# Weights' products ahead of what waits for VectorE within an attention step, and products of a zero tile where there are none

## The chip, the cores and the metric

One core of a Trainium2 chip runs the whole program in one launch. TensorE (PE) does the matrix products and transposes, VectorE (DVE) and ScalarE (ACT) read their results from PSUM, GpSimd (POOL) and SyncE (SP) issue the transfers. The metric is the device time of one execution in microseconds; 916.21 is the median of three runs of the kernel before (915.81 to 922.91).

## The reference

Three pieces run one after the other. First an attention over 2 x 8 heads of 768 positions and 64 dimensions, in which a query sees only the keys whose six signs under a random projection agree with its own:

```
mask   = q_bucket[:, :, :, None] == k_bucket[:, :, None, :]
scores = np.where(mask, scale * q @ k.T, -1e9)
attn   = exp(scores - max) ; attn = attn / (sum(attn) + 1e-09) ; out = attn @ v
```

Its output, 1536 x 512, goes through x = (h * tanh(softplus(h))) @ w_out with h = x @ w_in (2048 wide), and then through ((x @ w1) * (x @ w2)) @ w3 @ w_out (1024 wide). The last two matrices are multiplied with one another by the kernel (w3 @ w_out), and this product doesn't depend on the attention.

## The kernel before, in words

All products run on fp32 split into a high and a low part, in three passes. The attention is a loop over 96 steps n (line 865), pinned in the order in which it is written (`pin`, line 830). Six steps, n = 6j to 6j + 5, make one half pair of heads j; below, the position of a step is n mod 6. A step does the scores of one tile of 128 queries (`scores`, L540, tile ts, two PSUM banks), the row maximum (`maxima`, L551 and L554, VectorE), the exponential (`expo`, L562, ScalarE), and, for the half pair before, transposes of the exponentials (`unit`, L605, tile et, copied to etf in L612 by either ScalarE or VectorE) and products with the values (`av`, L620, tile pv, positions 2 to 4).

Other work hangs in named slots of a step, filled with `at(n, slot, fn)` and emptied with `run(n, slot)` in the order of lines 868 to 886: "la" (ScalarE copies), "un" and "av", "lv" (VectorE work that frees a bank), then "pe", "ea", "ev", "dm". Slot "pe" holds on TensorE: `qk_transpose` (L470, tile tqk) at positions 2 and 3, `bits_mm` (L500, tile tb) at positions 4 and 5, `rb_mm` (L587, tile rb) and, from n = 24 to n = 66, `w3_trans` (L678, tile w3p) at position 0. The tiles ts, tqk, tb and w3p share one ring of two PSUM buffers (tag "s"), so a later one waits until an earlier one has been read: tb at position 5 waits for `bits_dve` (L509) of position 5 to read the tb of position 4. rb waits for the reciprocal of `norm` (L574, L577), which runs in slot "lv" behind the copies of et and behind L509.

The weights' products are `wp_mm` (L703, tile wacc, the product w3 @ w_out; n = 26 to 73; 2, 2, 1, 6, 4 and 9 products at positions 2, 3, 4, 5, 0 and 1) and `h_early` (L334, tile hps, the first products of h; from n = 83; 4 or 8 a step). Both sit in slot "pe" too, and both write the one bank of tag "w". In the steps 0 to 25, and 74 to 82, there are none. TensorE takes its instructions in the order written. Behind the loop comes the block phase: three blocks of 512 rows through both networks. In the first block the weights are loaded as 64-bit numbers, one MB a chunk, by transfers that GpSimd issues (`load64`, L81), decoded by ScalarE and VectorE (L89, L96, L99, L107), and written back for the later blocks (L218).

Of the kernel before, what the change touches and what calls it, by code (L numbers as in the profile page):

```python
# [18 lines left out]
F32 = mybir.dt.float32  # L19
FR = mybir.dt.float32r  # L20
# [14 lines left out]
def kernel(  # L35
# [14 lines left out]
    nc = tc.nc  # L50
# [14 lines left out]
    const = ctx.enter_context(tc.tile_pool(name="const", bufs=1))  # L65
    big = ctx.enter_context(tc.tile_pool(name="big", bufs=2))
    strm = ctx.enter_context(tc.tile_pool(name="strm", bufs=2))
    ps = ctx.enter_context(tc.tile_pool(name="ps", bufs=1, space=PSUM))
# [8 lines left out]
    identr = const.tile([128, 128], FR, tag="identr", name="identr")  # L77
# [250 lines left out]
    def h_half(n, j, f, o, m0=0, m1=None):  # L328
        w, xh = weight(n, "wi", j), xhl[n]
        m1 = 3 * KD if m1 is None else m1  # L330
        for m in range(m0, m1):
            kk, i = divmod(m, 3)
            ws, xs = PASS[i]
            nc.tensor.matmul(  # L334
                o, lhsT=w[:, ws, kk, f * 128:(f + 1) * 128], rhs=xh[xs][:, kk, :],
                start=(m == 0), stop=(m == 3 * KD - 1),
            )
# [14 lines left out]
    def h_early(n, j, f, m0, m1):  # L352
        if m0 == 0:
            wh[0] = ps.tile([128, 512], F32, tag="w", name="hps1")
        h_half(n, j, f, wh[0], m0, m1)
# [32 lines left out]

    nc.scalar.preload_act_table_set("natural_log_exp_and_others")
    make_identity(nc, ident)  # L390
    zr = strm.tile([128, 512], FR, tag="xi", name="zr", bufs=2)
    nc.vector.memset(zr.bitcast(F32), 0.0)
    nc.scalar.copy(out=identr, in_=ident)

# [128 lines left out]
    for r in range(3):  # L523
        t = pa.tile([128, 6, 6], F32, tag=f"st{r}", name="st", bufs=1)
# [24 lines left out]
    def maxima(j, i):  # L549
        s = stats[j % 3]  # L550
        nc.vector.tensor_reduce(  # L551
            out=s[:, i, 1:2], in_=sc[j, i][:, :, 0:HS], axis=AX.XY, op=ALU.max, negate=True
        )
        nc.vector.scalar_tensor_tensor(  # L554
            out=s[:, i, 2:4], in0=s[:, i, 1:2].to_broadcast([128, 2]), scalar=THR,
            in1=s[:, i, 0:2], op0=ALU.is_le, op1=ALU.mult,
        )
# [14 lines left out]
    def norm(j):  # L572
        s = stats[j % 3]
        nc.vector.tensor_scalar(  # L574
            out=s[:, :, 4], in0=s[:, :, 4], scalar1=1e-9, scalar2=None, op0=ALU.add
        )
        nc.vector.reciprocal(out=s[:, :, 5], in_=s[:, :, 4])  # L577
# [4 lines left out]
    def rb_mm(j):  # L582
        s = stats[j % 3]
        t = rbs[j] = ps.tile([128, 512], F32, tag="p", name="rb")
        for ci in range(CH):
            for e in range(2):
                nc.tensor.matmul(  # L587
                    t[e * D:(e + 1) * D, ci * 128:(ci + 1) * 128],
                    lhsT=s[:, e * CH + ci, 5:6].to_broadcast([128, D]),
                    rhs=ident, start=True, stop=True,  # L590
                )

    def rb_act(j):
        t = rbs[j]
        rbs[j] = pa.tile([128, HS], F32, tag="rb", name="rb", bufs=2)
        nc.scalar.copy(out=rbs[j], in_=t[:, 0:HS])
# [5 lines left out]
    def unit(j, e, kt):  # L602
        t = ps.tile([128, 512], F32, tag="et", name="et", bufs=2)
        for ci in range(CH):
            nc.tensor.transpose(  # L605
                t[:, ci * 128:(ci + 1) * 128],
                E[j, e * CH + ci][:, kt * 128:(kt + 1) * 128],
                ident,
            )
        f = pa.tile([128, HS], F32, tag="etf", name="etf", bufs=NR)  # L610
        act = kt % 2 == 0 or (e == 0 and kt == 3)
        (nc.scalar.copy if act else nc.vector.tensor_copy)(out=f, in_=t[:, 0:HS])  # L612
        eth[j, e, kt] = f

    def av(j, kt):
        p = j // 2
        if kt == 0:
            pv[j] = ps.tile([128, 512], F32, tag="p", name="pv")
        for e in range(2):
            nc.tensor.matmul(  # L620
                pv[j][e * D:(e + 1) * D, 0:HS],
                lhsT=raws[p, "v"][:, e, kt, :],
                rhs=eth.pop((j, e, kt)),
                start=(kt == 0),
                stop=(kt == C - 1),
            )

    def x_out(j):
        p, a = divmod(j, 2)
        b, hp = divmod(p, H // 2)  # L630
        o = pa.tile([128, HS], F32, tag="xo", name="xo", bufs=2)
        nc.vector.tensor_mul(out=o, in0=pv.pop(j)[:, 0:HS], in1=rbs.pop(j))
        c0 = b * S + a * HS
        nc.sync.dma_start(out=x_d[hp * 128:(hp + 1) * 128, c0:c0 + HS], in_=o)
        blocks_done.add((p, a))
# [16 lines left out]
    def pre_a(nm, i):  # L652
        pre[nm, i] = decode_a(pre[nm, i])

    def pre_b(nm, i):
        pre[nm, i] = decode_b1(pre[nm, i])

    def pre_c(nm, i):
        pre[nm, i] = decode_b2(pre[nm, i])
        x = PRE.index((nm, i)) + 2  # L660
        if x < len(PRE):
            pre_load(x)
# [34 lines left out]
    def wp_mm(f, n0, n1):  # L697
        if n0 == 0:
            wacc[f] = ps.tile([128, 512], F32, tag="w", name="wacc")
        for n in range(n0, n1):  # L700
            g, s = divmod(n, 3)
            ws, rs = PASS[s]
            nc.tensor.matmul(  # L703
                wacc[f], lhsT=w3t[f][:, ws, g, :], rhs=wo2[rs][:, g, :],
                start=(n == 0), stop=(n == 3 * GT - 1),
            )
# [6 lines left out]

    slots = {}

    def at(n, where, fn):
        slots.setdefault((n, where), []).append(fn)

    def run(n, where):
        for fn in slots.pop((n, where), []):
            fn()
# [28 lines left out]
    for j in range(NJ):  # L752
        s = 6 * j
        for m in range(3):
            for kt in (2 * m, 2 * m + 1):
                at(s + 4 + m, "un", lambda j=j, kt=kt: unit(j, 0, kt))
                at(s + 7 + m, "un", lambda j=j, kt=kt: unit(j, 1, kt))
                at(s + 8 + m, "av", lambda j=j, kt=kt: av(j, kt))
        at(s + 6, "lv", lambda j=j: norm(j))
        at(s + 6, "pe", lambda j=j: rb_mm(j))  # L760
        at(s + 7, "la", lambda j=j: rb_act(j))
        at(s + 11, "lv", lambda j=j: x_out(j))
# [7 lines left out]
    for f in range(GT):  # L770
        n = 24 + 6 * f
        na, nb, nc_ = (n - 6, n - 4, n - 3) if f else (17, 20, 21)
        at(na, "ea", lambda f=f: pre_a(3, f))
        at(nb, "ev", lambda f=f: pre_b(3, f))
        at(nc_, "ev", lambda f=f: pre_c(3, f))
        at(n, "pe", lambda f=f: w3_trans(f))
        at(n + 1, "la", lambda f=f: w3_hi(f))
        at(n + 1, "lv", lambda f=f: w3_lo(f))
        m = 0
        for k_ in range(n + 2, n + 8):  # L780
            m1 = m + MM[k_ % 6]
            at(k_, "pe", lambda f=f, m=m, m1=m1: wp_mm(f, m, m1))
            m = m1
        assert m == 3 * GT
        at(n + 8, "la", lambda f=f: wp_out(f))
# [20 lines left out]
    n = 83  # L806
    for jj in range(3):
        for f in range(2):
            m = 0
            while m < 12:  # L810
                m1 = min(12, m + (4 if n % 6 in (2, 3, 4) or n == 83 else 8))
                at(n, "pe", lambda jj=jj, f=f, m=m, m1=m1: h_early(0, jj, f, m, m1))
                m = m1
                n += 1
            at(n, "la", lambda jj=jj, f=f: h_keep(0, jj, f))
    HEND = n

    def warm(n):
        t = ps.tile([128, 512], F32, tag="p", name="warm")
        for _ in range(n):  # L820
            nc.tensor.matmul(t, lhsT=zr[:, 0:128], rhs=zr, start=True, stop=True)

    def keep_warm(n, src):
        t = ps.tile([128, 512], F32, tag="p", name="warm")
        for _ in range(n):
            nc.tensor.matmul(t[:, 0:HS], lhsT=identr, rhs=src, start=True, stop=True)
# [38 lines left out]
    for n in range(max(NS + 6, HEND + 2)):  # L865
        j, i = divmod(n, 6)
        mark = len(nc.cur_bb.bb.instructions)
        run(n, "pr")
        if n < NS:
            scores(j, i)  # L870
        run(n, "la")
        if n < NS:
            maxima(j, i)
        run(n, "un")
        run(n, "av")
        run(n, "lv")
        if n < NS:
            expo(j, i)
        if n == 0:
            for x in range(2):  # L880
                with tc.issue_after(next(
                    i for i in reversed(nc.cur_bb.bb.instructions) if i.engine == nc.scalar.engine
                )):
                    pre_load(x)
        for w in ("pe", "ea", "ev", "dm"):
            run(n, w)
        pin(mark)
# [164 lines left out]
```

## Time and profile before

| | us |
|---|---|
| median of three runs | 916.21 |
| profiled execution | 920.4 |
| its span, first to last instruction | 918.6 |
| steps 0 to 95 (attention) | about 12 to 450 of the span |
| block phase | about 450 to the end |

The profiled execution is one of its own, 4.2 us above the median. PE busy times are from modelled ends of pipelined products, so the start of the next instruction is the better mark for how long one takes; "idle before" names the stretch in which an engine had nothing running, with what released it. [...]

### The profile page before, as it was taken

What the parts mean: (1) busy time and instruction counts of PE and PEld (TensorE: products, weight loads), DVE (VectorE), ACT (ScalarE), POOL (GpSimd) and SP (SyncE); (2) the same over time, 40 slices, a digit from 0 to 9 for tenths busy, and PEclk for the clock granted to TensorE, in tenths of its full rate; (3) what the DMA queues carried; (4) which work ended last, traced back from release to release, by engine and by line L of the source; (5) the groups of instructions that cost most, each with busy time, mean ns of one, the idle gap of its engine ahead of it and who ended that gap; (6) DMA issues with size and microseconds to landing.
All of it is one profiled execution on the core that took longest, in us unless ns stands there. A gap on an engine that the chain in (4) does not pass through costs nothing.

```text
span 918.6 us, 10516 instructions
## 1 busy us (share of the span) xinstructions
PE 830.0 (90%) x4145; PEld 648.7 (71%) x4145; DVE 512.4 (56%) x711; ACT 459.9 (50%) x691; POOL 74.6 (8%) x131
## 2 busy tenths in 40 slices
PE   6778868888888898788999999999999999999998
PEld 4655656566666666556778778888888888888886
DVE  5477756666655756767689877432354434334321
ACT  4556645566645675657856554333344323334221
POOL 1000000000000000001022211100101101110000
PEclk8588979999999999999999999999999999999999
DMA  5112313131031331326098864424233224232101
GB/s 177 52 54 81 117 55 107 67 118 58 26 113 55 118 103 36 115 89 214 9 329 301 293 231 183 142 94 152 95 110 97 92 92 137 95 107 75 46 24 47
DMA packets 34594, 103.46 MB, mean 113 GB/s; under 512 B 3184, under 2 KB 11632, under 8 KB 33520
## 3 DMA queue, kind: packets, MB, share of 16 engines
q0 software_dynamic: 20928, 81.80, 26.3%
q1 hardware_dynamic: 13472, 20.85, 6.6%
q8 instruction: 33, 0.54, 0.2%
q14 instruction: 17, 0.14, 0.1%
q10 hardware_dynamic: 144, 0.13, 0.0%
HBM read 81.79 MB, written 20.97 MB: 112 GB/s over the span
## 4 chain that ended last, share of the span: by engine, by line
PE 71%; DVE 14%; issue 5%; DMA 5%; ACT 4%; POOL 1%; SPq 0%; ACTq 0%; DVEq 0%; POOLq 0%
PE abp L941 14%; PE hps L334 10%; PE x2a L914 10%; PE ts L540 8%; PE oac L965 7%; PE pv L620 6%; PE wacc L703 5%; DVE st L551 4%; PE et L605 4%; PE tb L500 3%; DMA raw<-in_moe_w_dram 2%; PE rb L587 2%; DMA raw<-in_moe_w_out_dram 2%; DVE qa L509 2%; DVE ka L509 2%
## 5 line engine op out<-in xcount | busy, mean ns | idle before, releaser
L551 DVE TENSOR_REDUCE st<-ts 128x1 f32<-128x768 f32 x96 | 91.9, 957 | 151.3 <-PE ts L540 151.3
L941 PE MATMUL abp<-x2hl,hl 128*128 128x512 f32 x576 | 139.3, 398 | 2.1 <-ACT mh L347 2.1
L334 PE MATMUL hps<-xhl,hl 128*128 128x512 f32 x552 | 135.8, 400 | 0.0
L914 PE MATMUL x2a<-ghl,hl 128*128 128x512 f32 x552 | 130.6, 394 | 1.2 <-DVE ghl L379 1.1
L941 PEld LDWEIGHTS abp<-x2hl,hl 128*128 128x128 f32 x576 | 109.4, 190 | 28.4 <-ACT mh L347 2.5
L269 DVE TENSOR_TENSOR hl<-f,hl 128x1024 fp32r<-128x1024 f32 x60 | 73.4, 1224 | 91.5 <-ACT hl L264 91.5
L334 PEld LDWEIGHTS hps<-xhl,hl 128*128 128x128 f32 x552 | 104.2, 191 | 26.6 <-issue 3.5
L914 PEld LDWEIGHTS x2a<-ghl,hl 128*128 128x128 f32 x552 | 103.6, 188 | 25.9 <-DVE ghl L379 2.0
L562 ACT ACTIVATE E<-ts,st 128x768 f32<-128x768 f32 x96 | 95.3, 993 | 27.9 <-DVE st L554 26.5
L612 ACT COPY etf<-et 128x384 f32<-128x384 f32 x112 | 51.9, 478 | 85.0 <-PE et L605 84.4
L605 PE MATMUL et<-ident,E 128*128 128x128 f32 x576 | 85.0, 287 | 0.0
L605 PEld LDWEIGHTS et<-ident,E 128*128 128x128 f32 x576 | 74.4, 149 | 4.5 <-ACT etf L612 0.2
L264 ACT CAST hl<-f 128x1024 fp32r<-128x1024 f32 x60 | 62.8, 1047 | 28.9 <-PE abp L941 12.0
L620 PE MATMUL pv<-etf,rv 128*64 128x384 f32 x384 | 74.5, 511 | 0.0
L540 PE MATMUL ts<-ka,qa 76*128 76x384 f32 x192 | 59.2, 393 | 12.7 <-ACT E L562 10.9
L965 PE MATMUL oac<-hl,phl 128*128 128x512 f32 x288 | 69.8, 393 | 0.0
L965 PEld LDWEIGHTS oac<-hl,phl 128*128 128x128 f32 x288 | 54.2, 188 | 12.4
L703 PE MATMUL wacc<-wo,w3t 128*128 128x512 f32 x192 | 56.8, 419 | 0.0
L950 DVE TENSOR_TENSOR asb<-abp,asb 128x512 f32<-128x512 f32 x24 | 16.6, 692 | 71.6 <-ACT asb L949 71.6
L949 ACT COPY asb<-abp 128x512 f32<-128x512 f32 x24 | 14.1, 586 | 83.9 <-PE abp L941 83.9
L89 ACT ACTIVATE g<-raw 128x1024 f32<-128x1024 f32 x36 | 41.0, 1140 | 28.5 <-DMA raw<-in_moe_w_dram 9.6
L540 PE MATMUL ts<-kb,qb 128*128 128x384 f32 x192 | 54.3, 367 | 0.0
(108 smaller groups left out, 965.2 us busy)
## 6 DMA issues: line engine op xcount, KB each, us to landing
raw<-in_moe_w_dram POOLq DMA_DIRECT2D x16, 1024.0 KB, 6.1
raw<-in_moe_w_out_dram POOLq DMA_DIRECT2D x12, 1024.0 KB, 8.2
raw<-in_moe_w_in_dram POOLq DMA_DIRECT2D x8, 1024.0 KB, 6.8
f<-keep_wi POOLq DMA_DIRECT2D x16, 512.0 KB, 3.7
f<-keep_wo POOLq DMA_DIRECT2D x16, 512.0 KB, 3.7
f<-wp_d POOLq DMA_DIRECT2D x12, 512.0 KB, 4.0
keep_wi<-g POOLq DMA_DIRECT2D x8, 512.0 KB, 4.2
keep_wo<-g POOLq DMA_DIRECT2D x8, 512.0 KB, 3.1
```

The source lines that it names most:

```text
L264: nc.scalar.copy(out=hl[:, 0], in_=f)
L269: nc.vector.tensor_sub(out=hl[:, 1], in0=f, in1=hl[:, 0])
L334: nc.tensor.matmul(o, lhsT=w[:, ws, kk, f * 128:(f + 1) * 128], rhs=xh[xs][:, kk, :], start=(m == 0), stop=(m == 3 * KD - 1),)
L540: nc.tensor.matmul(t[:, a, 0:HS], lhsT=l[0:kk, qt * 128:(qt + 1) * 128], rhs=r[0:kk, a * HS:(a + 1) * HS], start=(l is qa), stop=(l is qb),)
L551: nc.vector.tensor_reduce(out=s[:, i, 1:2], in_=sc[j, i][:, :, 0:HS], axis=AX.XY, op=ALU.max, negate=True)
L562: nc.scalar.activation(out=e.rearrange("p (a n) -> p a n", a=2), in_=sc.pop((j, i))[:, :, 0:HS], func=AF.Exp, scale=s[:, i, 2:3], bias=s[: ...
L605: nc.tensor.transpose(t[:, ci * 128:(ci + 1) * 128], E[j, e * CH + ci][:, kt * 128:(kt + 1) * 128], ident,)
L620: nc.tensor.matmul(pv[j][e * D:(e + 1) * D, 0:HS], lhsT=raws[p, "v"][:, e, kt, :], rhs=eth.pop((j, e, kt)), start=(kt == 0), stop=(kt == C ...
L703: nc.tensor.matmul(wacc[f], lhsT=w3t[f][:, ws, g, :], rhs=wo2[rs][:, g, :], start=(n == 0), stop=(n == 3 * GT - 1),)
L914: nc.tensor.matmul(x2a[n][d], lhsT=w[:, ws, f, d * 128:(d + 1) * 128], rhs=g[:, gs, f, :], start=(j == 0 and f == 0 and s == 0), stop=(j = ...
L941: nc.tensor.matmul(t[:, i, :], lhsT=ws_[i][:, ws, kk, (f % 2) * 128:(f % 2) * 128 + 128], rhs=xh[:, xs, kk, :], start=(m == 0), stop=(m == ...
L965: nc.tensor.matmul(oac[n][t], lhsT=g[:, gs, t * 128:(t + 1) * 128], rhs=w[:, ws, f % 2, :], start=(f == 0 and s == 0), stop=(f == FF2 // 1 ...
```

## The change

`wp_mm` and `h_early` move from slot "pe" to a new slot "mm", which is emptied behind "av", so ahead of the transposes, `bits_mm`, `rb_mm` and `w3_trans` of the same step. Slot "lv" moves ahead of "un" (on VectorE ahead of the copies of et), and `norm` gets a slot of its own, "nm", ahead of "lv". In the steps 0 to 25 `fill` puts products of 128 x 512 of a tile of zeros into the bank "w": 5 each in the steps 0 to 7, then 8, 8 and 4 at the positions 0, 1 and 5: 100 in all. The zero tile gets a place of its own.

```diff
-    zr = strm.tile([128, 512], FR, tag="xi", name="zr", bufs=2)
+    zr = const.tile([128, 512], FR, tag="zr", name="zr")
...
-        at(s + 6, "lv", lambda j=j: norm(j))
+        at(s + 6, "nm", lambda j=j: norm(j))
...
-            at(k_, "pe", lambda f=f, m=m, m1=m1: wp_mm(f, m, m1))
+            at(k_, "mm", lambda f=f, m=m, m1=m1: wp_mm(f, m, m1))
...
-                at(n, "pe", lambda jj=jj, f=f, m=m, m1=m1: h_early(0, jj, f, m, m1))
+                at(n, "mm", lambda jj=jj, f=f, m=m, m1=m1: h_early(0, jj, f, m, m1))
...
+    def fill(n):
+        if not n:
+            return
+        t = ps.tile([128, 512], F32, tag="w", name="warm")
+        for _ in range(n):
+            nc.tensor.matmul(t, lhsT=identr, rhs=zr, start=True, stop=True)
+
+    for n in range(26):
+        at(n, "mm", lambda n=n: fill(5 if n < 8 else (8, 8, 0, 0, 0, 4)[n % 6]))
...
+        run(n, "nm")
+        run(n, "lv")
         run(n, "un")
         run(n, "av")
-        run(n, "lv")
+        run(n, "mm")
```

TensorE, the steps 29 and 30 (positions 5 and 0), from behind the transposes et of step 29 to behind rb or up to it. Before:

```order
L500 MATMUL tb<-kb,psel 76x384 x4
L703 MATMUL wacc<-wo_0_108,w3t 128x512 x2
L703 MATMUL wacc<-wo_1_109,w3t 128x512
L703 MATMUL wacc<-wo_0_108,w3t 128x512 x2
L703 MATMUL wacc<-wo_1_109,w3t 128x512
L540 MATMUL ts<-ka,qa 128x384 x2
L540 MATMUL ts<-kb,qb 128x384 x2
L605 MATMUL et<-ident,E 128x128 x6
L587 MATMUL rb<-ident,st 64x128 x6
L703 MATMUL wacc<-wo_0_108,w3t 128x512 x2
L703 MATMUL wacc<-wo_1_109,w3t 128x512
L703 MATMUL wacc<-wo_0_108,w3t 128x512
```

With the change:

```order
L703 MATMUL wacc<-wo_0_108,w3t 128x512 x2
L703 MATMUL wacc<-wo_1_109,w3t 128x512
L703 MATMUL wacc<-wo_0_108,w3t 128x512 x2
L703 MATMUL wacc<-wo_1_109,w3t 128x512
L500 MATMUL tb<-kb,psel 76x384 x4
L540 MATMUL ts<-ka,qa 128x384 x2
L540 MATMUL ts<-kb,qb 128x384 x2
L605 MATMUL et<-ident,E 128x128 x6
L703 MATMUL wacc<-wo_0_108,w3t 128x512 x2
L703 MATMUL wacc<-wo_1_109,w3t 128x512
L703 MATMUL wacc<-wo_0_108,w3t 128x512
L587 MATMUL rb<-ident,st 64x128 x6
```

The six products wacc of position 5 now stand ahead of tb, and the four of position 0 ahead of rb.

VectorE, positions 0 and 1 of a half pair with w3_trans (L574 and L577 are `norm`, L509 reads tb, L689 reads w3p, L612 copies et). Before:

```order
L551 TENSOR_REDUCE st<-ts 128x1
L554 SCALAR_TENSOR_TENSOR st<-st 128x2
L612 COPY etf<-et 128x384
L509 TENSOR_SCALAR ka<-tb,ccol 12x768
L574 TENSOR_SCALAR st<-st 128x6
L577 RECIPROCAL st<-st 128x6
L551 TENSOR_REDUCE st<-ts 128x1
L554 SCALAR_TENSOR_TENSOR st<-st 128x2
L612 COPY etf<-et 128x384
L689 TENSOR_TENSOR w3t<-w3p,w3t 128x1024
```

With the change:

```order
L551 TENSOR_REDUCE st<-ts 128x1
L554 SCALAR_TENSOR_TENSOR st<-st 128x2
L574 TENSOR_SCALAR st<-st 128x6
L577 RECIPROCAL st<-st 128x6
L509 TENSOR_SCALAR ka<-tb,ccol 12x768
L612 COPY etf<-et 128x384
L551 TENSOR_REDUCE st<-ts 128x1
L554 SCALAR_TENSOR_TENSOR st<-st 128x2
L689 TENSOR_TENSOR w3t<-w3p,w3t 128x1024
L612 COPY etf<-et 128x384
```

The two instructions of `norm` go from third and fourth behind the maximum to directly behind it; the copy of et goes behind L509 and L689.

TensorE, the steps 17 to 19 (positions 5, 0 and 1), where the change adds products of zeros (L829). With the change:

```order
L605 MATMUL et<-ident,E 128x128 x6
L829 MATMUL warm<-zr,identr 128x512 x4
L500 MATMUL tb<-kb,psel 76x384 x4
L540 MATMUL ts<-ka,qa 128x384 x2
L540 MATMUL ts<-kb,qb 128x384 x2
L605 MATMUL et<-ident,E 128x128 x6
L829 MATMUL warm<-zr,identr 128x512 x8
L587 MATMUL rb<-ident,st 64x128 x6
L540 MATMUL ts<-ka,qa 128x384 x2
L540 MATMUL ts<-kb,qb 128x384 x2
L605 MATMUL et<-ident,E 128x128 x6
L829 MATMUL warm<-zr,identr 128x512 x8
```

Before, the same rows stand there without the three of L829.

## Rows read from the trace of the kernel before

**Rows 1.** The page: TensorE's share of the span, and its granted clock in 40 slices.
```profile
PE 830.0 (90%) x4145; PEld 648.7 (71%) x4145; DVE 512.4 (56%) x711; ACT 459.9 (50%) x691; POOL 74.6 (8%) x131
...
PEclk8588979999999999999999999999999999999999
```
**Rows 2.** Windows: length, busy of PE, PEld, DVE, ACT, POOL, clock, DMA share, GB/s.
```profile
13.00:125.00 112.00, 84.16 (x444) 62.62 (x444) 71.68 (x115) 64.90 (x115) 2.53 (x4) 0.77 0.20 68
125.00:450.00 325.00, 274.90 (x1656) 207.74 (x1654) 205.94 (x332) 200.29 (x347) 12.41 (x20) 0.95 0.26 90
446.00:600.00 154.00, 150.77 (x671) 119.45 (x670) 114.64 (x122) 82.62 (x96) 29.69 (x47) 0.99 0.64 225
460.00:480.00 20.00, 20.00 (x94) 15.12 (x93) 15.46 (x17) 10.15 (x11) 4.58 (x7) 1.00 0.92 321
```
**Rows 3.** Waits of TensorE from 125 to 446: total, times, longest.
```profile
PE rb L587 <- DVE st L577: 28.7, 11, 2.8
PE tb L500 <- DVE qa L509: 17.9, 10, 1.8
PE ts L540 <- ACT E L562: 3.4, 4, 2.5
```
**Rows 4.** Waits of TensorE from 13 to 125.
```profile
PE tb L500 <- DVE qa L509: 7.6, 3, 3.3
...
PE rb L587 <- DVE st L577: 6.9, 3, 2.6
```
**Rows 5.** Timeline of TensorE, steps 35 and 36: start, length, instruction, idle before.
```profile
171.73 0.52 PE L540 MATMUL ts<-ka,qa 76*128 76x384 f32 x2
...
175.05 0.89 PE L500 MATMUL tb<-kb,psel 128*76 128x384 f32 x4 [1.79 <-DVE qa L509]
175.78 1.54 PE L703 MATMUL wacc<-wo,w3t 128*128 128x512 f32 x6
177.16 0.52 PE L540 MATMUL ts<-ka,qa 76*128 76x384 f32 x2
...
177.87 0.81 PE L605 MATMUL et<-ident,E 128*128 128x128 f32 x6
181.26 0.88 PE L587 MATMUL rb<-ident,st 128*64 128x128 f32 x12 [2.58 <-DVE st L577]
182.07 1.19 PE L703 MATMUL wacc<-wo,w3t 128*128 128x512 f32 x4
183.10 1.03 PE L678 MATMUL w3p<-ident,g 128*128 128x128 f32 x8
183.89 0.60 PE L540 MATMUL ts<-ka,qa 76*128 76x384 f32 x2
```
**Rows 6.** Timeline of VectorE in step 36.
```profile
179.06 0.16 DVE L554 SCALAR_TENSOR_TENSOR st<-st 128x2 f32<-128x2 f32 x1
179.14 0.55 DVE L612 COPY etf<-et 128x384 f32<-128x384 f32 x1
179.70 1.07 DVE L509 TENSOR_SCALAR ka<-tb,ccol 12x768 fp32r<-12x768 f32 x1
180.81 0.17 DVE L574 TENSOR_SCALAR st<-st 128x6 f32<-128x6 f32 x1
181.02 0.19 DVE L577 RECIPROCAL st<-st 128x6 f32<-128x6 f32 x1
```
**Rows 7.** Timeline of ScalarE in step 36.
```profile
179.25 0.99 ACT L562 ACTIVATE E<-ts,st 128x768 f32<-128x768 f32 x1 [0.38 <-DVE st L554]
```
**Rows 8.** Timeline of TensorE in step 66, at half clock.
```profile
323.88 1.91 PE L678 MATMUL w3p<-ident,g 128*128 128x128 f32 x8
```
**Rows 9.** Timeline of TensorE in step 84.
```profile
403.38 2.95 PE L334 MATMUL hps<-xhl,hl 128*128 128x512 f32 x8
```
**Rows 10.** Lines of VectorE from 125 to 450: count, busy, mean ns.
```profile
L689 DVE TENSOR_TENSOR w3t<-w3p,w3t 128x1024 fp32r<-128x1024 f32 x8 | 9.7, 1215 | 0.1
L107 DVE SCALAR_TENSOR_TENSOR g<-g,raw 128x1024 int32<-128x1024 int32 x14 | 17.0, 1218 | 0.0
```
**Rows 11.** The page's DMA issues: count, KB each, median us to landing.
```profile
raw<-in_moe_w_out_dram POOLq DMA_DIRECT2D x12, 1024.0 KB, 8.2
```

## The prediction

> **What bounds the kernel now.** I read the page first: TensorE is busy 90% of the span, and its clock is below 9 tenths only in the first slices [rows 1]. Then the windows: from 446 on TensorE works without a gap worth naming (150.77 of 154 us), so the block phase is bound by its products, and nothing in the change takes any of them away. The attention is different: from 125 to 450 TensorE is busy 274.90 of 325 us at a mean clock of 0.95, from 13 to 125 84.16 of 112 us at 0.77 [rows 2]. So up to 50 us of idle time and some lost clock lie in the second stretch. The waits say for whom: 28.7 us before rb for the reciprocal (11 times), 17.9 us before tb for L509 (10 times), 3.4 us before ts for the exponential [rows 3]. The timeline of two steps shows the pattern: at position 5 tb waits 1.79 us with six weights' products queued behind it; at position 0 rb waits 2.58 us with four behind it [rows 5]. Those products depend on nothing in the step. They are what could have run.
>
> **The change, part by part.**
>
> *Position 5.* The six products of wacc take 177.16 - 175.78 = 1.38 us, 0.23 each [rows 5]. Ahead of tb they fill 1.38 of the 1.79 us; tb is still released by L509, so 0.41 us of waiting stays. Eight steps have these six products (n = 29, 35, ..., 71): 8 x 1.38 = 11.0. Step 83 has four of hps there: 0.9. Step 77 has none: 0. Sum 11.9 of the 17.9 us.
>
> *Position 0.* Two edits act together. `norm` goes directly behind L554, so its end moves from 181.21 to 179.22 + 0.40 = 179.62, which is 2.46 us after the scores begin at 177.16 [rows 5, 6]; it loses the copy (0.55) and L509 (1.07) ahead of it. The four products take 183.10 - 182.07 = 1.03 us and go behind et, which ends 181.26 - 2.58 = 178.68, 1.52 after the scores: they end at 2.55 [rows 5]. The reciprocal is there by then, and the whole 2.58 goes. Next in the queue is w3p: in the new order it takes the bank that the exponential frees, at 180.24, that is 3.08 [rows 7], against 2.55 + 0.81 = 3.36 on TensorE, so no wait. The scores of position 1 need L509, which ends at 2.46 + 1.07 + a few hundredths = 3.6, against 3.36 + 0.79 = 4.15: no wait. So the step falls from 183.89 - 177.16 = 6.73 to 4.15 us. Eight steps (30, 36, ..., 72) give 8 x 2.58 = 20.6. Step 84 has eight products there (8 x 0.23 = 1.84): all of 2.58. Step 90 waits up to 2.84 [rows 3], and its products need the bank "w" copied out first: I count 2.3. Step 78 has no products, only the earlier `norm`: rb comes 1.62 earlier, but the next scores wait for L509, so 1.3. Sum 26.8 of 28.7.
>
> *What is late next.* On VectorE the copy of et at position 0 ends 1.47 us later (0.40 + 1.07), 3.6 + 0.55 = 4.15 after the scores begin; the transposes that need its bank come 1.1 us after the next scores, at 5.2. At position 1 it stands behind L689 (1.215 us, [rows 10]), with as little effect by the same count. At positions 2 to 4 the moved products only change places with a tqk or tb that TensorE did not wait for: nothing. I cost these moves at nothing; if that cover fails, the price is the first rival.
>
> *The clock.* [...] It does cost: behind the long wait of step 66 the eight transposes of w3p took 1.91 us instead of 1.03 [rows 5, 8], and the eight products of step 84 2.95 us instead of some 1.84 [rows 9]. Both follow directly on a wait at position 0 that the change closes. [...] What speaks for less: the same wait of 2.58 us in step 36 was followed by a w3p at full clock [rows 5], so an idle stretch of this length does not decide it alone. [...]
>
> *The zero products.* [...] In these steps the path is mostly scores, maximum, exponential, next scores, of which TensorE's speed is a part only. [...]
>
> *Block phase.* It starts earlier with the same program, but its loads run at a DMA share of 0.92 at the start [rows 2], and the order in which GpSimd issues loads and write-backs there shifts by a few places. TensorE lost 3.2 us there before; I add 2, between 0 and 5.
>
> **Sum.** 11.9 + 26.8 + 13 + 7 - 2 = 56.7, so 57 us off the profiled execution: 920.4 - 57 = 863. The median stands 4.2 us under that execution, so the forecast for a median is 859 us.
>
> **The rivals.**
>
> 1. *VectorE becomes the bound.* It is busy 205.94 of 325 us [rows 2]; in 275 us that is 75%. If the later copies of et hold up the transposes after all, the price is 16 x 1.47 at position 0 and 8 x 1.215 at position 1, 33 us: 892. Against it: the slack of 1.1 us above, and VectorE idle ahead of most maxima.
>
> 2. *The zero products don't lift the clock.* [...] For it: half speed lasted a whole slice there [rows 1] although TensorE was far from idle.
>
> 3. *Slower: one load in flight.* In the first block 20 chunks are still to be loaded, and a load stands in GpSimd's queue behind write-backs that wait for VectorE. Two in flight hide a landing of 8.2 us [rows 11] behind products of 24 x 0.23 = 5.5 us. If the new order leaves one in flight, a chunk costs 8.2 plus at least one decode pass of 1.22 [rows 10], 9.4, so 3.9 more than its products. From 15 such chunks on (15 x 3.9 = 58) the gain is gone; all 20 give 859 + 78 = 937. Against it: only 3.2 us idle there before, and the same buffers. [...]
>
> [...]
>
> That the change does not do what it says is ruled out by the order of the instructions, as far as places go.
>
> **How the numbers follow.** Forecast 0.62, rival 1 0.15, rival 2 0.08, rival 3 0.05, rival 4 0.10. The likeliest case spans about 850 to 870. The range of 846 to 888 leaves out rival 3, rival 2, the upper half of rival 1 and some of rival 4: about 2 in 10. A measurement of this kernel tells 1% (9 us) from no change; all cases but rival 3 lie below 907. Faster 0.94; within 1%, rival 3 with 10 to 17 chunks or two rivals at once, 0.03; slower 0.03.
>
> **What would show it.** Position 0 with w3p at about 4.2 us between scores, position 5 at about 4.05; waits before rb near zero in steps 30 to 72 and tb at 0.4; a clock of 0.98 or more through steps 24 to 73; the block phase as long as before. Wrong would be: waits of et for the copies on VectorE, steps 2 to 7 longer than the about 4 us of before, half clock through the early slices, or waits for loads behind the attention.

## The result: 859.1 us, and where the 57 us went

The changed kernel takes 859.11 us (median of 4 runs, 857.37 to 863.43) against 919.56 of the kernel before beside it (4 runs, 915.81 to 923.48): a ratio of 0.9349, 95% interval 0.9287 to 0.9412. The forecast was 859; against the median of three runs that it started from, 916.21, the change takes 57.1 us off. Of the 17 runs of the kernel before that stand beside the experiments 5 to 7, two lie over 1.5% above its fastest, count as slow and are left out of the figures below. The profiled execution took 863.43 us with a span of 861.7; the sum of the prediction, made against one profiled execution, gave 863.

The page of the changed kernel, TensorE's share and its clock in 40 slices, as in [rows 1]:

```profile
PE 825.7 (96%) x4245; PEld 643.9 (75%) x4245; DVE 513.5 (60%) x711; ACT 456.0 (53%) x691; POOL 75.3 (9%) x131
...
PEclk9799999999999999999999999999999999999999
```

TensorE's busy time is nearly that of before (830.0) although it holds 100 products more; its share went from 90% to 96%. The windows of the changed kernel (length, busy of PE, PEld, DVE, ACT, POOL, clock, DMA share, GB/s). Step 24 starts at 113.79 and step 95 at 388.58 now, before at 117.78 and 446.18:

```profile
13.00:112.00 99.00, 85.52 (x494) 63.99 (x492) 66.98 (x108) 62.33 (x111) 2.54 (x4) 0.93 0.22 75
112.00:390.00 278.00, 266.66 (x1689) 198.81 (x1690) 207.89 (x337) 197.07 (x347) 12.45 (x20) 1.00 0.32 105
390.00:545.00 155.00, 151.06 (x669) 119.70 (x669) 116.36 (x123) 81.68 (x97) 30.31 (x47) 0.99 0.64 223
```

Against [rows 2], the 50 us in which TensorE was idle from 125 to 450 have become 11, at a clock of 1.00 instead of 0.95, and VectorE is busy 75% of the stretch. The block phase looks as before. TensorE's waits from 112 to 390 (total, times, longest), against [rows 3]:

```profile
PE tb L500 <- DVE qa L509: 7.5, 11, 1.8
...
PE rb L587 <- DVE st L577: 0.9, 1, 0.9
PE hps L334 <- ACT mh L361: 0.8, 1, 0.8
```

Of 28.7 us before rb 0.9 are left, in step 78, which has no products to put there. Of the 7.5 us before tb, 1.55 lie in step 23, ahead of the stretch of [rows 3]; so 6.0 are left of 17.9, as the prediction's 17.9 - 11.9 has it. The timeline of TensorE, steps 35 and 36 (start, length, instruction, idle before), as in [rows 5]:

```profile
158.92 0.51 PE L540 MATMUL ts<-ka,qa 76*128 76x384 f32 x2
...
160.19 1.62 PE L703 MATMUL wacc<-wo,w3t 128*128 128x512 f32 x6
162.23 0.89 PE L500 MATMUL tb<-kb,psel 128*76 128x384 f32 x4 [0.42 <-DVE qa L509]
162.96 0.52 PE L540 MATMUL ts<-ka,qa 76*128 76x384 f32 x2
163.31 0.52 PE L540 MATMUL ts<-kb,qb 128*128 128x384 f32 x2
163.67 0.82 PE L605 MATMUL et<-ident,E 128*128 128x128 f32 x6
164.24 1.17 PE L703 MATMUL wacc<-wo,w3t 128*128 128x512 f32 x4
165.38 0.88 PE L587 MATMUL rb<-ident,st 128*64 128x128 f32 x12
166.19 1.09 PE L678 MATMUL w3p<-ident,g 128*128 128x128 f32 x8
167.04 0.60 PE L540 MATMUL ts<-ka,qa 76*128 76x384 f32 x2
```

Position 5 takes 162.96 - 158.92 = 4.04 us (5.43 before) and keeps a wait of 0.42 before tb; position 0 takes 167.04 - 162.96 = 4.08 (6.73 before), and rb follows its products without a wait. Why, the timeline of VectorE in steps 36 and 37 shows, against [rows 6]:

```profile
164.86 0.16 DVE L554 SCALAR_TENSOR_TENSOR st<-st 128x2 f32<-128x2 f32 x1
164.94 0.16 DVE L574 TENSOR_SCALAR st<-st 128x6 f32<-128x6 f32 x1
165.14 0.19 DVE L577 RECIPROCAL st<-st 128x6 f32<-128x6 f32 x1
165.36 1.08 DVE L509 TENSOR_SCALAR ka<-tb,ccol 12x768 fp32r<-12x768 f32 x1
166.47 0.56 DVE L612 COPY etf<-et 128x384 f32<-128x384 f32 x1
168.03 0.96 DVE L551 TENSOR_REDUCE st<-ts 128x1 f32<-128x768 f32 x1 [1.00 <-PE ts L540]
```

The reciprocal ends at 165.33, before the products do; L509 and the copy of et end at 166.44 and 167.03, and VectorE then still waits 1.00 us for the next scores. So nothing is late behind them.

### The profile page after: what moved, and what is told of

Same layout as the page of the kernel before. It is cut to its first block, busy times and chain, and to the rows that moved or that the text cites. A ratio compares the mean times of both kernels' runs of the same rounds, so it can differ in the third digit from the quotient of the medians.

```text
span 861.7 us, 10711 instructions
## 1 busy us (share of the span) xinstructions
PE 825.7 (96%) x4245; PEld 643.9 (75%) x4245; DVE 513.5 (60%) x711; ACT 456.0 (53%) x691; POOL 75.3 (9%) x131
## 4 chain that ended last, share of the span: by engine, by line
PE 73%; DVE 11%; ACT 7%; DMA 5%; issue 4%; POOL 1%; SPq 0%; ACTq 0%; DVEq 0%; POOLq 0%
PE abp L954 15%; PE x2a L927 10%; PE hps L334 10%; PE oac L978 8%; PE ts L540 8%; PE pv L620 6%; PE et L605 4%; PE wacc L703 4%; DMA raw<-in_moe_w_dram 3%; DVE st L551 3%; PE tb L500 2%; DVE qa L509 2%; ACT E L562 2%; PE rb L587 1%; ACT g L89 1%
## 5 line engine op out<-in xcount | busy, mean ns | idle before, releaser
L334 PE MATMUL hps<-xhl,hl 128*128 128x512 f32 x552 | 133.3, 395 | 0.8 <-ACT mh L361 0.8
L954 PEld LDWEIGHTS abp<-x2hl,hl 128*128 128x128 f32 x576 | 109.4, 190 | 28.7 <-ACT mh L347 2.9
L612 ACT COPY etf<-et 128x384 f32<-128x384 f32 x112 | 52.1, 480 | 62.2 <-PE et L605 61.8
L605 PE MATMUL et<-ident,E 128*128 128x128 f32 x576 | 80.0, 275 | 0.0
L605 PEld LDWEIGHTS et<-ident,E 128*128 128x128 f32 x576 | 69.5, 142 | 4.9 <-issue 0.8
L620 PE MATMUL pv<-etf,rv 128*64 128x384 f32 x384 | 72.3, 498 | 0.0
L540 PE MATMUL ts<-ka,qa 76*128 76x384 f32 x192 | 55.0, 368 | 10.4 <-ACT E L562 7.4
L379 DVE TENSOR_TENSOR ghl<-mh,ghl 128x1024 fp32r<-128x1024 f32 x24 | 29.4, 1223 | 39.0 <-ACT ghl L378 38.9
```

Source lines behind the costliest of these rows:

```text
L334: nc.tensor.matmul(o, lhsT=w[:, ws, kk, f * 128:(f + 1) * 128], rhs=xh[xs][:, kk, :], start=(m == 0), stop=(m == 3 * KD - 1),)
L540: nc.tensor.matmul(t[:, a, 0:HS], lhsT=l[0:kk, qt * 128:(qt + 1) * 128], rhs=r[0:kk, a * HS:(a + 1) * HS], start=(l is qa), stop=(l is qb),)
L605: nc.tensor.transpose(t[:, ci * 128:(ci + 1) * 128], E[j, e * CH + ci][:, kt * 128:(kt + 1) * 128], ident,)
L620: nc.tensor.matmul(pv[j][e * D:(e + 1) * D, 0:HS], lhsT=raws[p, "v"][:, e, kt, :], rhs=eth.pop((j, e, kt)), start=(kt == 0), stop=(kt == C ...
L954: nc.tensor.matmul(t[:, i, :], lhsT=ws_[i][:, ws, kk, (f % 2) * 128:(f % 2) * 128 + 128], rhs=xh[:, xs, kk, :], start=(m == 0), stop=(m == ...
```

## The experiments

Each kernel was compared with the kernel before on its own chip; ratios are to that. A step is measured from the start of its scores to the start of the next. The edits of the experiments 1, 6, 7 and 8 are shown against the change, those of 2 to 5 against the kernel before.

**1. The change without the products of zeros.**

```diff
-    for n in range(26):
-        at(n, "mm", lambda n=n: fill(5 if n < 8 else (8, 8, 0, 0, 0, 4)[n % 6]))
```

> The change without the 100 zero products. Theory (the gain is closed waits at positions 5 and 0, the clock follows by itself): position 5 stays at 4.04 us and position 0 at 4.09 us in the steps 30 to 71, only the first 26 steps lose what the fill gave, 4 us up to step 24 and up to 5 at steps 24 and 26: 863 to 869 us. Rival (the fill brings the clock up and the later steps live on it): w3p at 1.9 us and position 0 near 5 again in some half pairs, clock 0.95 behind step 26, 875 us or more.

Measured: 861.34 us (860.9 to 863.88), ratio 0.9405 (0.9372 to 0.9437). Its windows up to and behind 112:

```profile
13.00:112.00 99.00, 73.02 (x411) 52.98 (x411) 67.62 (x109) 62.62 (x112) 2.54 (x4) 0.83 0.23 76
112.00:390.00 278.00, 265.62 (x1669) 197.26 (x1670) 206.38 (x336) 195.76 (x345) 12.45 (x20) 0.99 0.31 105
```

The early clock falls from 0.93 to 0.83, and yet step 24 starts at 112.73, earlier than with the zeros (113.79). Behind it only step 26 loses by their absence (5.59 us instead of 4.00), and step 95 starts at 389.07 instead of 388.58: as they were placed, the 100 products are worth half a microsecond between these two executions. By the medians it is 2 to 4 us (861.34 against 859.11 above and 857.76 at the end of this section), on different chips and with intervals of the ratios that overlap. Either way it is less than I had expected here (863 to 869 us without them): what made the early steps shorter must in the main be something else.

**2. The kernel before with the products of zeros alone**, at the same places, behind the old slot "lv" (`fill` and the place of the zero tile as in the change).

```diff
+    for n in range(26):
+        at(n, "mm", lambda n=n: fill(5 if n < 8 else (8, 8, 0, 0, 0, 4)[n % 6]))
...
         run(n, "lv")
+        run(n, "mm")
```

> The kernel before with the 100 zero products alone; weights' products, L509, L689 and the norm stay where they were. Theory: waits of 2.58 us before rb and 1.79 before tb stay from step 26 on, with their passages at half clock; the first 26 steps are 2 to 8 us shorter: 908 to 915 us. Rival (clock by fill carries on): position 0 without half clock in the steps 54 to 72, 900 us or less.

Measured: 914.13 us (10 runs, 905.36 to 916.73), ratio 0.9958 (0.9924 to 0.9991). Step 30 starts 8.4 us earlier than before, but most of it is gone by step 54 (0.7): half pairs that were at full clock before now fall to half. The timeline of TensorE in step 36 of this kernel:

```profile
174.48 1.55 PE L587 MATMUL rb<-ident,st 128*64 128x128 f32 x12 [2.58 <-DVE st L577]
175.96 2.08 PE L703 MATMUL wacc<-wo,w3t 128*128 128x512 f32 x4
177.84 1.91 PE L678 MATMUL w3p<-ident,g 128*128 128x128 f32 x8
```

It is the wait of 2.58 us of [rows 5], after the same work, and there rb took 0.88 and w3p 1.03. Which half pairs fall to half clock is thus no property of the step.

**3. VectorE's order alone** (`norm` first, "lv" ahead of the copies; products where they were, no zeros).

```diff
-        at(s + 6, "lv", lambda j=j: norm(j))
+        at(s + 6, "nm", lambda j=j: norm(j))
...
+        run(n, "nm")
+        run(n, "lv")
         run(n, "un")
         run(n, "av")
-        run(n, "lv")
```

> Only VectorE's order is changed (norm first, then L509 and L689, then the copies of et); products stay behind tb and rb, no zero products. Theory: position 0 falls by 1.62 (the copy and L509 no longer ahead of the norm) to 5.1 us, position 5 stays at 5.43; 8 x 1.62 and some 1.3 at seven other half pairs, with half of the 13 us of clock: 22 to 30 us off, 887 to 897. Rival (later copies hold up the transposes): position 1 longer than 3.5 us and et waiting for L612, 905 or more.

Measured: 887.28 us (885.41 to 888.48), ratio 0.9678 (0.965 to 0.9705). The wait before rb in step 36, where the products of TensorE wait for no copy of et; and the waits before rb from 13 to 125, against [rows 4]:

```profile
168.33 0.88 PE L587 MATMUL rb<-ident,st 128*64 128x128 f32 x12 [0.90 <-DVE st L577]
```

```profile
PE rb L587 <- DVE st L577: 1.5, 3, 0.9
```

Position 0 takes 5.06 us instead of 6.73. Step 26 starts 8.3 us earlier than before: here is the gain of the early steps. 7.1 us of it lie in the steps 12 to 14, 18 to 20 and 24, where an rb stands.

**4. The products alone** ("mm" behind the old order of VectorE, no zeros).

```diff
-            at(k_, "pe", lambda f=f, m=m, m1=m1: wp_mm(f, m, m1))
+            at(k_, "mm", lambda f=f, m=m, m1=m1: wp_mm(f, m, m1))
...
         run(n, "lv")
+        run(n, "mm")
```

(`h_early` likewise.)

> Only the weights' products move ahead of tb and rb; VectorE's order as before, no zero products. Theory: position 5 at 4.04; at position 0 the four products fill 1.03 of the 2.58, so 1.55 us of waiting stays and the step takes 5.7; 11.9 + 8.2 + 3.7 at steps 84 and 90, and some of the clock: 24 to 32 us off, 885 to 893. The savings of this and of VectorE's order alone add up to that of both (within 5 us). Rival (either alone opens the whole wait): each takes 40 us or more off.

Measured: 886.97 us (885.93 to 888.68), ratio 0.9678 (0.9651 to 0.9705). Position 5 takes 4.04 us; in step 36 the wait before rb stays 1.65 us, because the reciprocal still comes behind the copy and L509:

```profile
174.43 0.88 PE L587 MATMUL rb<-ident,st 128*64 128x128 f32 x12 [1.65 <-DVE st L577]
```

At step 95 the two halves are 29.8 and 34.1 us ahead, together 63.9, and the pair of them (experiment 1) 57.1. I had expected the sums to agree within 5 us; between the traces they are 6.8 apart, by the medians 3.8 (29.4 and 29.7 against 55.4). The traces differ by more because of the clock: in the steps 54 to 72 and 84 before had some 7.5 us of half clock that either half is rid of, so that they count twice, and each half has falls of its own in other steps (65, 71 and 83 in experiment 3, 78 here) that take 6 us back; the rest lies in the main at step 26 and ahead of it.

**5. The clock alone.** The kernel before, its order untouched, with ten products of zeros ahead of rb at position 0 of the steps 30 to 90 (`fill` as in the change, but into the bank of rb and pv, tag "p", where the expectation says a bank of their own).

```diff
+    for n in range(30, 96, 6):
+        at(n, "mm", lambda: fill(10))
...
+        run(n, "mm")
```

> The kernel before, its order untouched, with ten products of zeros ahead of rb at position 0 of steps 30, 36, ..., 90, into a bank of their own: TensorE is busy during the wait of 2.58 us, but no work of the program moves. Theory (idle time ahead of rb is what lets the clock fall, and the fall costs time by itself): position 0 at 6.73 us in all of the steps 30 to 72 instead of up to 8.12, w3p 1.03 us each time, a clock of 0.98 or more from 125 on, and the 13 us of my clock term less than before: 899 to 907 us. Rival (the clock falls for another reason, or its fall hits only waiting): 912 us or more, with a clock of 0.95 to 0.96 from 125 on.

Measured: 909.78 us (10 runs, 905.33 to 912.17; before beside it 915.18, 15 runs, 906.23 to 919.66), ratio 0.9929 (0.9897 to 0.9962): between the two expectations. A window of the attention; step 66, against [rows 8]; and step 47:

```profile
125.00:440.00 315.00, 289.27 (x1755) 218.23 (x1754) 204.44 (x332) 199.24 (x344) 12.46 (x20) 0.99 0.27 92
```

```profile
316.81 2.52 PE L829 MATMUL warm<-zr,identr 128*128 128x512 f32 x10
319.73 0.88 PE L587 MATMUL rb<-ident,st 128*64 128x128 f32 x12 [0.39 <-DVE st L577]
320.53 1.19 PE L703 MATMUL wacc<-wo,w3t 128*128 128x512 f32 x4
321.56 1.04 PE L678 MATMUL w3p<-ident,g 128*128 128x128 f32 x8
```

```profile
229.06 1.31 PE L500 MATMUL tb<-kb,psel 128*76 128x384 f32 x4 [1.79 <-DVE qa L509]
230.16 2.74 PE L703 MATMUL wacc<-wo,w3t 128*128 128x512 f32 x6
```

The steps go nearly as the first expectation has them: with ten products of zeros ahead of rb, every position 0 of steps 30 to 66 takes 6.82 to 6.84 us, where before they took 6.73 to 8.12, w3p 1.04 instead of 1.91, and the granted clock from 125 on is 0.99 instead of 0.95. The size is smaller. Against the profiled execution of before, step 95 is 8.65 us ahead; 1.29 of it was there at the start of step 30, ahead of the first of these products (step 26 ran faster in this execution). Against the gain stand 0.10 us in each of the eleven steps (the ten products end before the reciprocal does, but rb starts 0.15 us behind it instead of 0.06; why stays open), and one step that fell still: step 47 took 6.98 instead of 5.43, its wacc x6 2.74 us behind the wait of 1.79. So from step 30 on falls of the clock cost that execution 8.65 - 1.29 + 1.1 + 1.55 = 10.0 us. The medians are 5.4 us apart: all 15 executions of before were granted more clock than the profiled one (0.955 to 0.973 over the span, against 0.953).

**6. The products of zeros only where a wait stood.** The two windows of experiment 1 leave a question: the clock rose by 0.10 and next to nothing came of it. The change's steps 18 and 19:

```profile
89.90 0.52 PE L540 MATMUL ts<-ka,qa 76*128 76x384 f32 x2
...
91.19 2.08 PE L829 MATMUL warm<-zr,identr 128*128 128x512 f32 x8
93.20 0.88 PE L587 MATMUL rb<-ident,st 128*64 128x128 f32 x12
94.00 0.62 PE L540 MATMUL ts<-ka,qa 76*128 76x384 f32 x2
...
95.39 2.10 PE L829 MATMUL warm<-zr,identr 128*128 128x512 f32 x8
97.32 0.51 PE L540 MATMUL ts<-ka,qa 76*128 76x384 f32 x2
```

rb starts 3.30 us after the scores, although the reciprocal ends 2.37 us after them, at 92.27, and position 1 holds 2 us of zeros where nothing waits. The edit leaves them out there, and sizes the others to the waits:

```diff
-    for n in range(26):
-        at(n, "mm", lambda n=n: fill(5 if n < 8 else (8, 8, 0, 0, 0, 4)[n % 6]))
+    for n, z in {0: 5, 1: 5, 2: 11, 3: 5, 4: 4, 5: 5, 6: 7, 7: 5, 11: 14, 23: 10, 25: 8}.items():
+        at(n, "mm", lambda z=z: fill(z))
```

> The change with the products of zeros put only where a wait stood in these steps, sized to it: 74 instead of 100, in steps 0 to 7, 11, 23 and 25, none at positions 0 and 1 of the steps 12 to 24. Theory (there the products of zeros lie on TensorE's own path and lengthen steps, since the earlier norm has already closed those waits): steps 12 to 14 take about 10.5 us together instead of 11.9, steps 18 to 20 about 9.2 instead of 10.9, step 3 stays at about 3.3 to 4.0 at full clock, step 26 at 4.0; some 5 to 9 us less than the change, 850 to 854 us. Rival (what is saved in these steps is lost to a clock that falls in other steps): within 4 us of the change, 855 to 863.

Measured: 852.15 us (6 runs, 851.41 to 855.32), ratio 0.9315 (0.9275 to 0.9355); the change itself on the same chip 857.76 (4 runs, 856.18 to 860.41). The ranges don't meet: faster by 5.6 us. Its window up to 112 and its steps 18 and 19:

```profile
13.00:112.00 99.00, 84.71 (x523) 63.17 (x522) 71.15 (x116) 65.06 (x115) 2.52 (x4) 0.98 0.23 77
```

```profile
84.31 0.52 PE L540 MATMUL ts<-ka,qa 76*128 76x384 f32 x2
...
86.75 0.88 PE L587 MATMUL rb<-ident,st 128*64 128x128 f32 x12 [0.90 <-DVE st L577]
87.55 0.61 PE L540 MATMUL ts<-ka,qa 76*128 76x384 f32 x2
...
88.92 0.59 PE L540 MATMUL ts<-ka,qa 76*128 76x384 f32 x2
```

rb starts 2.44 us after the scores, with a wait of 0.90, and the step is 0.86 shorter for it; position 1 takes 1.37 instead of 3.32, of which position 2 gives 1.2 back (4.61 instead of 3.43). Steps 12 to 14 take 9.3 us instead of 11.9 (10.5 expected), steps 18 to 20 9.2 instead of 10.9, step 3 4.15 (3.3 to 4.0 expected). The clock is even higher, 0.98.

**7. One product more at position 5.** Experiment 6 with `MM = (4, 8, 2, 2, 1, 7)` in place of `(4, 9, 2, 2, 1, 6)`.

> The run before in this list (zero products only where a wait stood), and one product wacc more at position 5, taken from position 1 (8 and 7 instead of 9 and 6). Theory (0.41 us of waiting ahead of tb at position 5 is still open to work that depends on nothing): position 5 stays at 4.04 us with a wait of some 0.18 before tb, position 1 falls from about 3.5 to 3.3, eight half pairs x 0.2 = 1.6 us less than that run: 848 to 853 us. Rival (position 1 is bound by VectorE and ScalarE, not by its products): the same time as that run within 0.5 us, and position 1 at 3.5.

Measured: 850.74 us (6 runs, 849.58 to 852.3), ratio 0.9295 (0.9256 to 0.9334): the fastest of all, 7.0 us below the change beside it. Position 5 in step 35:

```profile
151.96 1.84 PE L703 MATMUL wacc<-wo,w3t 128*128 128x512 f32 x7
153.99 0.89 PE L500 MATMUL tb<-kb,psel 128*76 128x384 f32 x4 [0.19 <-DVE qa L509]
```

The wait is 0.19, position 5 still 4.03 and position 1 3.31 instead of 3.50; but position 2 grows from some 3.94 to some 4.04. Steps 30 to 77 take 186.09 us instead of 187.04, so 0.95 less instead of 1.6. The medians differ by 1.4, with overlapping runs: the step is shown by the trace, its size in the total is not.

**8. `norm` first, and nothing else of VectorE's new order** (no zeros; "lv" behind the copies as before).

```diff
         run(n, "nm")
-        run(n, "lv")
         run(n, "un")
         run(n, "av")
+        run(n, "lv")
         run(n, "mm")
```

> The change without its products of zeros, and of VectorE's new order only the half that concerns rb: norm directly behind the maximum; L509 and L689 stand behind the copies of et again, as before. Theory (position 0 needs norm early and nothing else; L509 only has to end before the next scores, and has slack there): position 0 at 4.1 to 4.3 us, position 5 at 4.04, 861 to 865 us, as without the zero products alone (861.3). Rival (freeing the bank early is half of the gain at position 0, since the next scores or w3p wait for L509): position 0 at 4.7 us or more in the steps 30 to 66, 866 to 872 us.

Measured: 861.45 us (859.64 to 862.14), ratio 0.9414 (0.9379 to 0.9449), the time of experiment 1. VectorE in step 36:

```profile
165.68 0.19 DVE L577 RECIPROCAL st<-st 128x6 f32<-128x6 f32 x1
165.78 0.52 DVE L612 COPY etf<-et 128x384 f32<-128x384 f32 x1
166.32 1.07 DVE L509 TENSOR_SCALAR ka<-tb,ccol 12x768 fp32r<-12x768 f32 x1
```

The copy stands ahead of L509 again, and position 0 takes 4.09 us as in experiment 1. Of the order on VectorE the two small instructions of `norm` are the whole effect that shows; that the bank is freed first brought nothing in these runs.

The changed kernel run again beside experiments 6 and 7:

> The change itself, beside the others on one chip: 857 to 863 us. Any theory expects the same; it is the measure for the first two runs of this list.

Measured: 857.76 us. Its block phase, from step 95 to the end of the span, took 470.0 us and the first profile's 473.1, so 3 us there differ between two executions of one kernel.

## Why the prediction was right, and which terms were off

The sum was made for the profiled execution of before, whose span of 918.6 us became 861.7:

| stretch | predicted | measured |
|---|---|---|
| steps 0 to 25, put down to the zero products | -7 | -6.6 |
| position 5, n = 29 to 83 | -11.9 | -12.0 |
| position 0, n = 30 to 90, at full clock | -26.8 | -27.6 |
| clock from 125 on | -13 | -11.4 |
| block phase | +2 | +0.6 |
| sum | -56.7 | -57.0 |

*Position 5.* Eight steps fell from 5.43 to 4.04 (8 x 1.39 = 11.1) and step 83 from 5.07 to 4.14 (0.9). tb still waits for L509, as the step said.

*Position 0.* Seven times 2.64 (6.73 to 4.09), and 2.71, 1.68, 2.74 and 1.94 in the steps 72, 78, 84 and 90, with the lengths of experiment 5, less 0.10, as those at full clock. Step 90, put at 2.3, got 1.94: the wait moved to hps, 0.8 us for the copy that frees its bank. Both edits are needed, as the step said: experiments 3 and 4 leave 0.90 and 1.65 us.

*The clock.* No run shows the 13 us that the sum takes for it. 11.4 is what remains of the 51.0 us from step 26 on when the two terms above are taken off, 9.1 of it from step 30 on; experiment 5 gives 10.0 there by another way. The 11.4 are net of about 1 us that the prediction put at nothing: with the products moved, position 4 became 0.11 us longer (3.89 to 4.00) in the steps 34 to 70 and step 27 0.53 (3.98 to 4.51). So 13 was near for this execution and too much for a median one, where experiment 5 gains 5.4. It is the term that belongs to one execution: in the ones profiled here the falls lie in different steps, and the spread of before goes with the clock (906.23 us at 0.973, 919.66 at 0.955), 13 us against the 3 or 4 of experiments 6 and 7 (at 0.991 to 1.000). That sum and median both came out is in part luck: it rests on the two profiled executions lying equally far, some 4 us, above a median, that of before above its median of three runs (with the fourth, 919.56, it is 0.8).

*The zero products.* The right amount for the wrong reason. No run shows the 7 us that the sum takes for them: the stretch became 6.6 shorter, but without them it becomes 7.7 shorter (step 26 starts at 121.71, before at 129.40) and with VectorE's order alone 8.3. The waits before rb in this stretch, 6.9 us in [rows 4], did not need the fill: the earlier `norm` closes them but for 1.5 (experiment 3), as it does later, and my term for position 0 had left them out. The fill itself brought 0.5 us between these executions, 2 to 4 by the medians: its good side (the early clock, 0.93 against 0.83) was for the most part taken back, at positions 0 and 1 of the steps 12 to 24, where it stands on TensorE's own path, and in step 3. Put where waits stand, it brings 389.07 - 381.53 = 7.5 us at step 95.

*The block phase.* +0.6, within what two executions of one kernel differ by; nothing is to be explained.

*The rivals.* VectorE as the bound: refuted, no wait of TensorE's products for a copy of et in any of these traces (in the whole trace of the change the loads of the weights waited for VectorE's copies of et 0.3 us ahead of et and 1.0 ahead of rb), and the order of copies and L509 makes no difference (experiment 8). A clock that the zeros don't lift: refuted, 0.83 from 13 to 112 us without (experiment 1) and 0.93 with them. One load in flight in the first block: refuted, 155 us at a DMA share of 0.64 with TensorE busy for 151.06 of them. More coming back: not here, but experiment 6 shows that on the zero products 5.6 us more were to be had by the medians, 7.1 at step 95.

*What would show it.* The clock of 1.00, rb and tb came as said. Steps 2 to 7 did not: step 3 fell to half clock with its own five zeros in it (2.33 us; granted clock 0.50 from 25.0 to 29.5) and took 6.06 instead of 3.99, step 4 4.67 instead of 4.00; steps 2, 5, 6 and 7 became shorter, and the six together 28.6 instead of 30.3.

## What to carry to other kernels

Where an engine that works in order waits for another, look behind the waiting instruction for work that doesn't depend on it and count it: the time filled was here about the smaller of the wait and that work (at position 5 1.37 us of a wait of 1.79, by products of 1.38; ahead of rb in experiment 4 0.93 of 2.58, by products of 1.03), and the other engine's own order decided the rest (two instructions of 0.2 us each, moved ahead of two of 0.55 and 1.07). Work that only keeps an engine busy paid here where that engine waits (74 products, 7.5 us at step 95) and cost time where it doesn't (in the steps 18 to 20 1.6 us for 16 products of 3.9), so size it to each wait, and after the other edits, which may have closed it. A gain in clock that is read from one execution is that execution's (here 10.0 us, and 5.4 between the medians): weigh it against the spread of the runs.

## What the runs showed of the hardware

The same wait of 2.58 us, behind the same instructions, is followed by full clock in step 36 of before (rb 0.88 us, w3p 1.03; granted clock 1.00 from 181.3 to 184.0) and by half clock in step 66 of before (w3p 1.91; 0.50 from 323.9 to 325.4) and in step 36 of experiment 2 (rb 1.55, w3p 1.91). A wait of 1.79 us, followed by full clock in step 35 of before (wacc x6 in 1.54), is followed by half clock in step 47 of experiment 5 (2.74). So in these runs the length of a wait alone did not decide the clock behind it; what did is not shown.

With 74 products of a tile of zeros the stretch from 13 to 112 us was granted a clock of 0.98 (experiment 6), without them 0.83 (experiment 1); with ten ahead of each rb the attention from 125 us on was granted 0.99 (experiment 5), without them 0.95 (before).
